# Reordering the start of a fused FFT filter and feed-forward kernel: first-FFT copies, load order, and the half-swaps of batch 1

## The chip, the cores and the metric

The kernel runs on one core of one Trainium2 chip. The metric is the device time of one execution in microseconds (us); lower is better. The engines are TensorE (PE, its weight loads apart as PEld), VectorE (DVE), ScalarE (ACT), GpSimd (POOL) and SyncE (SP, which here only issues transfers).

## The reference

An input x of shape (8, 3008, 256) is filtered along its second axis in the frequency domain, and every one of the 24064 resulting rows goes through a feed-forward block with a squared ReLU.

```python
X = np.fft.rfft(x, axis=1)                      # x: (8, 3008, 256)
Y = X * (filt_r + 1j * filt_i)[None, :, :]      # filter: (1505, 256)
y = np.fft.irfft(Y, n=3008, axis=1).reshape(24064, 256)
h = np.maximum(y @ w_in, 0.0)                   # w_in: (256, 2048)
out = h * h @ w_out                             # w_out: (2048, 256)
```

## The kernel before

**The transform.** The length 3008 is split as 64 x 47. One batch passes through stage A (a 47-point transform as matrix products with the constant in `sC0`), stage B (a 64-point transform with `sSB`, whose PSUM result is multiplied by the filter `sF` into `prod`), stage P (the inverse 64-point transform with `sSP`, copied to `ze` and written to the DRAM array `dZ`), and stage Y (the inverse 47-point transform of `zt`, which is read back from `dZ`, copied out as `yt`). Batches 1 to 7 also pass through a DRAM array `dU` between stages A and B, to bring another index onto the partitions. From batch 1 on, `unit_b` swaps the two halves of 64 partitions of `prod` by two copies into `yf`, and `unit_s` adds the other half of `prod` to it. For batch 1 these two copies run on POOL (lines 445 and 446), for batches 2 to 7 on DVE.

**The feed-forward block.** It works on 47 groups of 512 rows with 8 slots each. In a slot, `ffn_g1` multiplies `yt` by `sWin` into `psH` (line 542) and ACT applies the ReLU (line 546); DVE squares it (`ffn_sq`, line 550); `ffn_g2` multiplies an older group's `h` by `sWout` into `psO` (line 557). The FFT of batch 1 and later is spread over these slots by `fft_plan`, which gives each step a slot number `r` and a place in it. Batch 1 has `unit_b` in slots 14 to 33, `unit_p` two slots later, and also the rest of stage Y of batch 0. The last loop of the function writes the order out; every engine carries out its own instructions in this order, and each waits on semaphores for its operands and buffers.

**The prologue.** Before the first slot, batch 0 is transformed on its own. x of batch 0 is loaded in three parts (`load_wide`), cast to half precision (`cast_wide`), taken through stage A in turned form (`chunk_a0`, lines 395 to 405: eight steps, each with two PSUM banks `dt` 0 and 1), turned by products with an identity (`turn_u`, line 413, six steps), and the filter is brought into place by products with a selection matrix (`place_f`, lines 285 to 299, twelve steps, half of them after `turn_u` and mixed with stages B and P). A loop over `r` then does stages B and P of batch 0. `chunk_a` does three quarters of stage A of batch 1, and `unit_y(0, 0..3)` the first quarter of stage Y of batch 0, with which the first slots can start. `keep_warm` gives PE products of zeros while the first x loads.

**The queues.** Almost all transfers are issued by SP in program order; one that waits holds up all behind it. Each transfer also waits for the one eight places earlier, with which it shares a semaphore. The three `ze` buffers of a batch are reused: the fourth `ze` of batch 0 waits for the first write to `dZ`. The `prod` pool has three buffers, and the selection matrix `sPF` holds one of them until the filter is placed. PSUM tiles `psH`, `psF` and `psO` have two buffers each; a `psH` tile has two banks and counts as one tile for waits.

Of the kernel before, what the change touches and what calls it, by code (L numbers as in the profile page):

```python
# [111 lines left out]
def kernel(  # L112
# [9 lines left out]
    nc = tc.nc  # L122
# [10 lines left out]
    dPF = nc.inline_tensor(PF_np, name="cPF")  # L133
# [28 lines left out]
    def psO(name):  # L162
        return pps.tile([128, 2, 256], F32, tag="psO", name=name, bufs=2)

    def psH(name):
        return pps.tile([128, 2, 512], F32, tag="psH", name=name, bufs=2)
# [34 lines left out]


    sC0 = const.tile([128, 1472], F16, name="sC0")
    nc.scalar.dma_start(out=sC0, in_=dC0.ap())
    s0 = sC0[:, 0:576].rearrange("p (w q) -> p w q", q=96)
    s1 = sC0[:, 896:1472].rearrange("p (w q) -> p w q", q=96)
    sSA = sC0[0:94, 576:672]
    sSY = sC0[0:112, 672:766]
    ident = sC0[:, 768:896]
    sPF = p_prod.tile([128, 6, 128], F16, tag="prod", name="sPF")  # L210
    nc.scalar.dma_start(out=sPF, in_=dPF.ap().rearrange("p (w q) -> p w q", q=128))

    xw32, xw16 = {}, {}

# [6 lines left out]
        nc.sync.dma_start(out=t, in_=(v0[:, 0:8, :], v1, v0[:, 8:16, :])[k])  # L221
        xw32[(b, k)] = t

    def cast_wide(b, k, eng):
        t = p_x16.tile([128, 8, D], F16, tag="x16", name=f"xw16_{b}_{k}")
        for i in range(2):
            m = slice(4 * i, 4 * i + 4)
            eng.tensor_copy(out=t[:, m, :], in_=xw32[(b, k)][:, m, :])
        xw16[(b, k)] = t

    for k in range(3):
# [5 lines left out]
    def load_f(im):  # L237
        filt = filt_i if im else filt_r
        t = p_y.tile([128, QF], F32, tag="yt", name=f"f32_{im}")
        nc.sync.dma_start(out=t, in_=filt[0:1504, :].rearrange("a d -> (a d)")  # L240
                          .rearrange("(p e) -> p e", e=QF))
        f32s.append(t)

    load_f(0)
    load_f(1)
    nyq = p_out.tile([128, 2, D], F32, tag="ost", name="nyq")
    nc.gpsimd.memset(nyq, 0.0)
# [9 lines left out]
    zero = const.tile([128, 128], F16, name="zero")  # L257
    nc.vector.memset(zero, 0.0)

    def keep_warm(n):  # L260
        ps = psO("warm").rearrange("p a d -> p (a d)")
        for _ in range(n):
            nc.tensor.matmul(ps[:, 0:128], zero, zero, start=True, stop=True)

    nc.scalar.copy(out=zero[0:1, 0:1], in_=zero[0:1, 1:2])
    keep_warm(125)


    sF = const.tile([128, 2, NC, D], F16, name="sF")

    f16s = []

# [45 lines left out]
        nc.sync.dma_start(out=w32s[2][:, c, :],  # L318
                          in_=moe_w_out.rearrange("(jt r) c -> r jt c", r=128)[:, c, :])

    def cast_wout(k):
        c = slice(4 * k, 4 * k + 4)
        nc.gpsimd.tensor_copy(out=sWout[:, c, :], in_=w32s[2][:, c, :])


    x16s, us, uts, prods, zes, zts, yts = {}, {}, {}, {}, {}, {}, {}
# [57 lines left out]
    def chunk_a0(c):  # L384

        for k in range(2):
            for dt in range(2):
                if dt == 0:
                    banks, _ = bank_pair(f"psA_0_{c}_{k}")
                ps = banks[dt]  # L390
                for i in range(4):
                    m = 4 * k + i
                    o = ps[:, 96 * i:96 * i + 96]
                    d = slice(128 * dt, 128 * dt + 128)
                    nc.tensor.matmul(o, xw16[(0, 2 * (c % 2))][:, m, d], s0[:, c // 2, :],
                                     start=True, stop=False)
                    nc.tensor.matmul(o, xw16[(0, 1)][0:120, m, d], s0[0:120, 2 + c, :],
                                     start=False, stop=True)
                m = 32 * c + 16 * k
                o = uT[:, dt, :, m:m + 16].rearrange("p c (m q) -> p m c q", q=4)  # L400
                pv = ps[:, 0:384].rearrange("p (m c q) -> p m c q", m=4, q=4)
                if dt == 0:
                    nc.scalar.copy(out=o, in_=pv)
                else:
                    nc.vector.tensor_copy(out=o, in_=pv)
# [25 lines left out]
    def unit_b(b, p):  # L431
        ps = psF(f"psB_{b}_{p}")
        for i in range(2):
            nc.tensor.matmul(ps[:, i * D:(i + 1) * D], sSB[:, 2 * p + i, :],  # L434
                             uts[b][:, 2 * p + i, :], start=True, stop=True)
        prod = p_prod.tile([128, 2, 2, D], F16, tag="prod", name=f"prod_{b}_{p}")
        nc.vector.tensor_mul(  # L437
            out=prod,
            in0=ps.rearrange("p (a d) -> p a d", d=D).unsqueeze(1).to_broadcast([128, 2, 2, D]),
            in1=sF[:, :, 2 * p:2 * p + 2, :])  # L440
        prods[(b, p)] = prod
        if b > 0:
            yf = p_yf.tile([128, 2, D], F16, tag="yf", name=f"yf_{b}_{p}")
            swap = nc.gpsimd if b == 1 else nc.vector
            swap.tensor_copy(out=yf[0:64], in_=prod[64:128, 1])  # L445
            swap.tensor_copy(out=yf[64:128], in_=prod[0:64, 1])  # L446
            prods[(b, p)] = prod, yf

    def unit_s(b, p):
# [39 lines left out]
                              in_=v[48 * k:48 * k + 48, 8 * c:8 * c + 8, :])  # L489
        zts[(b, c)] = zt  # L490

    yps = {}

    def unit_y(b, n):

        g, dt = divmod(n, 2)
        if n == 0:
            yts[b] = p_y.tile([128, 2, S], F16, tag="yt", name=f"yt_{b}")
        zt = zts[(b, g // 2)]
        if not prologue[0]:  # L500
            ps = psF(f"psY_{b}_{n}")
        elif g % 2 == 0:
            ps = psF(f"psY_{b}_{n}") if dt == 0 else psO(f"psY_{b}_{n}").rearrange("p a d -> p (a d)")
        else:
            if dt == 0:
                yps[0] = psH(f"psY_{b}_{n}")
            ps = yps[0][:, dt, :]
        if prologue[0]:
            for k in range(2):
                nc.tensor.matmul(ps[:, 128 * k:128 * k + 128], zero, zero, start=True, stop=True)  # L510
        for jj in range(4):
            nc.tensor.matmul(ps[:, 94 * jj:94 * jj + 94],  # L512
                             zt[:, 4 * (g % 2) + jj, dt * 128:(dt + 1) * 128],
                             sSY, start=True, stop=True)
        r, t = g // 2 * 2, g % 2 * 4
        o = yts[b].rearrange("p d (r a t) -> p d r a t", r=8, t=8)[:, dt, r:r + 2, :, t:t + 4]
        pv = ps[:, 0:376].rearrange("p (j a i) -> p i a j", j=4, i=2)
        if dt == 0:
            nc.scalar.copy(out=o, in_=pv)  # L519
        else:  # L520
            nc.vector.tensor_copy(out=o, in_=pv)  # L521
# [62 lines left out]
    def fft_plan(b):  # L584

        plan = {}

        def put(r, place, f, *a):
            plan.setdefault((r, place), []).append((f, a))

        if b == 1:
            for n in range(4, 16):
                put(n - 1 if n < 8 else 10 + n // 2 if n < 12 else 4 * n - 31, n % 2,
                    unit_y, 0, n)
        t0 = 2 if b == 1 else 6
        for a in range(12 if b == 1 else 0, 16):
            put(t0 + a // 2, a % 2, unit_a, b, a)
        put(10 if b == 1 else 14, 1, read_u, b)
        t0 = 14 if b == 1 else 18
        for p in range(12):  # L600
            r = t0 + 19 * p // 11
            put(r, 0, unit_b, b, p)
            put(r, 0, unit_s, b, p)
            put(r + 2, 1, unit_p, b, p)
        t0 = 36 if b == 1 else 40
        for c in range(4):
            put(t0, 1, read_z, b, c)
        if b + 1 < B:
            for c in range(2):
                put(t0 - 13, 1, load_x, b + 1, c)  # L610
            for c in range(4):
                r = t0 - 8 + 3 * c
                put(r, 1, cast_x, b + 1, c)
                if c < 2:
                    put(r, 1, load_x, b + 1, c + 2)
        for n in range(16):
            if b == 1:
                put(38 + n // 2 if n > 3 else 39, n % 2, unit_y, b, n)
            else:
                put(44 + n // 2, n % 2, unit_y, b, n)  # L620
        return plan
# [4 lines left out]


    uT = p_h2.tile([128, 2, NC, 128], F16, tag="h2", name="uT")
    for k, eng in enumerate((nc.vector, nc.vector, nc.gpsimd)):
        cast_wide(0, k, eng)  # L630

    def load_const(t, d, k):
        c = slice(12 * k, 12 * k + 12)
# [19 lines left out]
    uts[0] = p_ut.tile([128, NC, D], F16, tag="ut", name="ut_0")  # L653
    for k in range(6):
        turn_u(k)
    for k in range(3):
        if k == 2:
            load_wout(0)
        load_wide(1, k)
        cast_wide(1, k, nc.gpsimd)  # L660
    load_wout(1)
    for k in range(4):
        cast_wout(k)
    for k, eng in enumerate((nc.vector, nc.scalar, nc.vector)):
        place_f(0, k, eng)
    place_f(1, 0, nc.scalar)
    for r in range(14):
        if r < 12:
            unit_b(0, r)
        if r < 10 and r % 2 == 0:  # L670
            place_f(1, r // 2 + 1, nc.scalar)
        if r < 6 and r % 2 == 1:
            place_f(0, r // 2 + 3, nc.scalar)
        if r >= 2:
            unit_p(0, r - 2)
        if r == 10:
            read_z(0, 0, (0,))
    read_z(0, 1, (0,))
    for c in (0, 2, 1):
        chunk_a(1, c)  # L680
    for c in range(2):
        read_z(0, c, (1,))
    for c in (0, 2, 1):
        write_u(1, c)
    for n in range(4):
# [53 lines left out]
```

## Time and profile before

| quantity | value |
|---|---|
| median of 5 runs | 821.2 us (817.61 to 822.67) |
| profiled execution, its own time | 819.99 us |
| its span in the profile | 818.2 us |
| PE busy | 787.7 us (96%) |
| DVE busy | 543.4 us (66%) |
| ACT busy | 554.2 us (68%) |
| POOL busy | 39.0 us (5%) |
| first ReLU of the feed-forward block (ACT, line 546) | 61.51 us from the span's start |
| the chain that ended last, by engine | PE 82%, DMA 10%, DVE 4%, POOL 2%, ACT 1% |

The profile is one execution, 1.8 us of whose time lies outside the span. "Busy" is the time in which an engine has an instruction under way. Where a row of a view ends in brackets, it gives the idle time of the engine before the instruction and what ended that idle time. A "window" is a stretch of the span in us from its start; the granted clock (PEclk) is the share of the full clock that TensorE had in it.

### The profile page before, as it was taken

To read this page: it belongs to the slowest core of one execution; us is meant where nothing else is said; L and a number is where in the kernel's file an instruction comes from. 1 tells how busy PE (TensorE), PEld (TensorE's weight loads), DVE (VectorE), ACT (ScalarE), POOL (GpSimd) and SP (SyncE) were. 2 spreads that over 40 slices of the span, in tenths; PEclk is the share of its full clock that TensorE was granted. 3 is DMA by queue.
4 is the path that set the end of the run, shared out by engine and by line. 5 is a ranking of instruction groups with operands and counts; after the bars stand their busy time and mean duration, and the time that the engine had idled before them with its cause. 6 is when DMAs were issued, how large, how long until landed. Compare 5 with 4: busy or idle time off the path is not lost.

```text
span 818.2 us, 14996 instructions
## 1 busy us (share of the span) xinstructions
PE 787.7 (96%) x6201; PEld 559.4 (68%) x6201; DVE 543.4 (66%) x868; ACT 554.2 (68%) x709; POOL 39.0 (5%) x53
## 2 busy tenths in 40 slices
PE   7879898999999999999999999999999999999998
PEld 7745565666677676776768667676767667676666
DVE  5755567558965699557985599656995579653442
ACT  2747565677777677676777767776776767766664
POOL 3520221000000000000000000000000000000000
PEclk9999999999999999999999999999999999999999
DMA  9893255534672554424572455715555242411111
GB/s 364 344 270 96 76 150 134 112 105 152 164 174 58 163 155 129 130 76 144 155 196 64 107 162 151 174 59 161 150 135 127 79 140 78 126 56 39 39 40 52
DMA packets 87948, 108.11 MB, mean 132 GB/s; under 512 B 6224, under 2 KB 78544, under 8 KB 83408
## 3 DMA queue, kind: packets, MB, share of 16 engines
q1 hardware_dynamic: 87528, 106.59, 45.3%
q8 instruction: 48, 0.79, 0.4%
q10 hardware_dynamic: 288, 0.57, 0.3%
q14 instruction: 20, 0.16, 0.1%
q0 software_dynamic: 64, 0.00, 0.0%
HBM read 58.90 MB, written 48.23 MB: 131 GB/s over the span
## 4 chain that ended last, share of the span: by engine, by line
PE 82%; DMA 10%; DVE 4%; POOL 2%; ACT 1%; issue 0%; ACTq 0%; POOLq 0%; DVEq 0%; SPq 0%
PE psO L557 36%; PE psH L542 35%; DMA ut<-dU 3%; DMA dZ<-ze 3%; PE psA L351 3%; PE psY L512 3%; PE psB L434 2%; PE psP L470 2%; DMA sSB<-cSB 2%; DMA zt<-dZ 2%; DVE prod L437 2%; DVE h L550 1%; DMA sPF<-cPF 1%; POOL yf L446 1%; POOL yf L445 1%; ACT h L546 1%
## 5 line engine op out<-in xcount | busy, mean ns | idle before, releaser
L546 ACT ACTIVATE h<-psH 128x1024 f16<-128x1024 f32 x376 | 385.1, 1025 | 196.1 <-PE psH L542 196.1
L542 PE MATMUL psH<-yt,sWin 128*128 128x512 f16 (+7 forms) x1728 | 388.6, 352 | 3.9 <-DVE yt L521 3.4
L557 PE MATMUL psO<-sWout,h 128*128 128x256 f16 x3008 | 389.6, 273 | 0.3 <-DVE h L550 0.3
L557 PEld LDWEIGHTS <-h 128*128 128x128 f16 x3008 | 290.9, 98 | 79.0 <-DVE h L550 0.6
L550 DVE TENSOR_TENSOR h<-h 128x1024 f16<-128x1024 f16 x376 | 254.0, 685 | 104.8 <-ACT h L546 103.2
L542 PEld LDWEIGHTS <-sWin 128*128 128x128 f16 x1728 | 159.8, 98 | 104.6 <-issue 6.4
L437 DVE TENSOR_TENSOR prod<-psB,sF 128x1024 f16<-128x1024 f32 x96 | 116.7, 1220 | 12.1 <-PE psB L434 8.9
L472 ACT CAST ze<-psP 128x512 f16<-128x512 f32 x96 | 55.9, 586 | 29.8 <-PE psP L470 22.9
L521 DVE CAST yt<-psY 128x376 f16<-128x376 f32 x64 | 35.0, 549 | 57.0 <-PE psY L512 56.7
L357 DVE CAST u<-psA 96x512 f16<-96x512 f32 x50 | 34.3, 687 | 47.6 <-PE psA L351 45.1
L564 ACT COPY ost<-psO 128x512 f32<-128x512 f32 x94 | 55.4, 589 | 9.1 <-PE psO L557 7.7
L452 DVE TENSOR_TENSOR yf<-prod,yf 128x512 f16<-128x512 f16 x84 | 35.7, 425 | 19.4 <-POOL yf L446 17.0
L512 PEld LDWEIGHTS <-zt 112*128 112x128 f16 x512 | 34.7, 97 | 15.3 <-issue 5.0
L512 PE MATMUL psY<-sC,zt 112*128 112x94 f16 x512 | 42.2, 205 | 2.9 <-DMA zt<-dZ 1.9
L434 PE MATMUL psB<-ut,sSB 128*128 128x256 f16 x192 | 36.8, 273 | 3.2 <-DVE prod L437 1.2
L351 PE MATMUL psA<-x,sC 94*96 94x512 f16 x96 | 36.6, 382 | 0.0
L470 PE MATMUL psP<-yf,sSP 128*128 128x256 f16 x168 | 32.6, 276 | 4.2 <-DVE prod L437 3.6
L434 PEld LDWEIGHTS <-sSB 128*128 128x128 f16 x192 | 18.7, 98 | 24.3 <-issue 5.7
L519 ACT CAST yt<-psY 128x376 f16<-128x376 f32 x64 | 29.8, 467 | 1.5 <-issue 1.0
L330 DVE CAST x<-x 94x2048 f16<-94x2048 f32 x24 | 29.2, 1217 | 0.0
L355 ACT CAST u<-psA 96x512 f16<-96x512 f32 x50 | 28.6, 572 | 0.0
L445 DVE COPY yf<-prod 64x512 f16<-64x512 f16 x72 | 20.8, 289 | 2.5
(59 smaller groups left out, 248.2 us busy)
## 6 DMA issues: line engine op xcount, KB each, us to landing
x<-in_x_dram SPq DMA_DIRECT2D x20, 768.0 KB
dZ<-ze SPq DMA_DIRECT2D x32, 384.0 KB
zt<-dZ SPq DMA_DIRECT2D x64, 192.0 KB
dU<-u SPq DMA_DIRECT2D x28, 384.0 KB
out_dram<-ost SPq DMA_DIRECT2D x32, 256.0 KB
out_dram<-ost SPq DMA_DIRECT2D x64, 128.0 KB
ut<-dU SPq DMA_DIRECT2D x7, 1024.0 KB
xw<-in_x_dram SPq DMA_DIRECT2D x6, 1024.0 KB
```

The costliest lines, as they stand in the source:

```text
L351: nc.tensor.matmul(ps[0:96, :], sSA, x16s[(b, c)][:, m, :], start=True, stop=True)
L434: nc.tensor.matmul(ps[:, i * D:(i + 1) * D], sSB[:, 2 * p + i, :], uts[b][:, 2 * p + i, :], start=True, stop=True)
L437: nc.vector.tensor_mul(out=prod, in0=ps.rearrange("p (a d) -> p a d", d=D).unsqueeze(1).to_broadcast([128, 2, 2, D]), in1=sF[:, :, 2 * p:2 ...
L452: nc.vector.tensor_add(out=yf, in0=prod[:, 0], in1=yf)
L470: nc.tensor.matmul(ps[:, i * D:(i + 1) * D], sSP[:, c2, :], prod[:, i, :], start=True, stop=True)
L472: nc.scalar.copy(out=zes[(b, c)][:, 2 * i6:2 * i6 + 2, :], in_=ps.rearrange("p (a d) -> p a d", d=D))
L512: nc.tensor.matmul(ps[:, 94 * jj:94 * jj + 94], zt[:, 4 * (g % 2) + jj, dt * 128:(dt + 1) * 128], sSY, start=True, stop=True)
L542: nc.tensor.matmul(ps[:, i, o:o + n], sWin[:, dt, jt * 128:(jt + 1) * 128], yts[b][:, dt, r:r + n], start=(dt == 0), stop=(dt == 1))
L546: nc.scalar.activation(out=h2[:, 2 * s:2 * s + 2, :], in_=ps, func=AF.Relu)
L550: nc.vector.tensor_mul(out=v, in0=v, in1=v)
L557: nc.tensor.matmul(pso[g][:, t % 2, :], h2s[g][:, jt, t * 128:(t + 1) * 128], sWout[:, jt, :], start=(jt == 0), stop=(jt == NJT - 1))
L564: nc.scalar.copy(out=ost, in_=pso[g])
```

## The change

The change has these parts:

- **Loads at the start.** The first transfer on ACT's queue carries only the 576 columns of `sC0` that `chunk_a0` reads. `sPF` and the other columns of `sC0` (identity and the constants of later stages) go to SP's queue, between the two halves of the filter.
- **Warm-up.** 26 products with 512 columns take the place of 125 with 128; DVE clears the operand first.
- **`cast_wide(0, 2)`.** DVE casts the first half and POOL the second; before, POOL cast both.
- **`chunk_a0`.** Where both banks are in one `psH` tile, both are copied out by the same engine (ACT and DVE in turn); before, ACT copied bank 0 and DVE bank 1 of every tile.
- **`turn_u` and `place_f`.** The first three steps of `place_f` come after steps 3, 4 and 5 of `turn_u`, on DVE, ACT and DVE; before, they came after the whole of `turn_u`.
- **Loads of x of batch 1 and of W_out.** These were issued before the writes of `dZ`; now they are issued in the loop over `r`, at r = 4, 7 and 10, and the second half of W_out after the reads of `zt` 0 and 1.
- **`cast_wout`.** The second half of W_out is cast by DVE in slots 4 and 5; before, POOL cast all of it.
- **`unit_y` in the prologue.** All four products use `psF` and `psO` tiles; before, two of them shared one `psH` tile.
- **Half-swaps.** The two copies into `yf` run on DVE for batch 1 too.

```diff
-    nc.scalar.dma_start(out=sC0, in_=dC0.ap())
+    nc.scalar.dma_start(out=sC0[:, 0:576], in_=dC0.ap()[:, 0:576])
...
-    nc.scalar.dma_start(out=sPF, in_=dPF.ap().rearrange("p (w q) -> p w q", q=128))
...
-    def cast_wide(b, k, eng):
+    def cast_wide(b, k, *engs):
...
-            eng.tensor_copy(out=t[:, m, :], in_=xw32[(b, k)][:, m, :])
+            engs[i].tensor_copy(out=t[:, m, :], in_=xw32[(b, k)][:, m, :])
...
     load_f(0)
+    nc.sync.dma_start(out=sPF, in_=dPF.ap().rearrange("p (w q) -> p w q", q=128))
+    nc.sync.dma_start(out=sC0[:, 576:1472], in_=dC0.ap()[:, 576:1472])
     load_f(1)
...
-    keep_warm(125)
...
+    nc.vector.memset(sF[:, 0, 0:2, :], 0.0)
+    ps = psO("warm").rearrange("p a d -> p (a d)")
+    for _ in range(26):
+        nc.tensor.matmul(ps, zero, sF[:, 0, 0:2, :], start=True, stop=True)
...
-    def cast_wout(k):
+    def cast_wout(k, eng):
...
         for k in range(2):
+            banks, groups = bank_pair(f"psA_0_{c}_{k}")
             for dt in range(2):
-                if dt == 0:
-                    banks, _ = bank_pair(f"psA_0_{c}_{k}")
...
-                if dt == 0:
+                if (pair_engine() is nc.scalar) if len(groups) == 1 else (dt == 0):
                     nc.scalar.copy(out=o, in_=pv)
...
-            swap = nc.gpsimd if b == 1 else nc.vector
-            swap.tensor_copy(out=yf[0:64], in_=prod[64:128, 1])
-            swap.tensor_copy(out=yf[64:128], in_=prod[0:64, 1])
+            nc.vector.tensor_copy(out=yf[0:64], in_=prod[64:128, 1])
+            nc.vector.tensor_copy(out=yf[64:128], in_=prod[0:64, 1])
...
-        elif g % 2 == 0:
+        else:
             ps = psF(f"psY_{b}_{n}") if dt == 0 else psO(f"psY_{b}_{n}").rearrange("p a d -> p (a d)")
-        else:
-            if dt == 0:
-                yps[0] = psH(f"psY_{b}_{n}")
-            ps = yps[0][:, dt, :]
...
+            for k in range(2, 4):
+                put(2 + k, 1, cast_wout, k, nc.vector)
...
-    for k, eng in enumerate((nc.vector, nc.vector, nc.gpsimd)):
-        cast_wide(0, k, eng)
+    for k in range(3):
+        cast_wide(0, k, nc.vector, nc.gpsimd if k == 2 else nc.vector)
...
         turn_u(k)
-    for k in range(3):
-        if k == 2:
-            load_wout(0)
-        load_wide(1, k)
-        cast_wide(1, k, nc.gpsimd)
-    load_wout(1)
-    for k in range(4):
-        cast_wout(k)
-    for k, eng in enumerate((nc.vector, nc.scalar, nc.vector)):
-        place_f(0, k, eng)
+        if k > 2:
+            place_f(0, k - 3, nc.vector if k % 2 else nc.scalar)
     place_f(1, 0, nc.scalar)
...
             unit_p(0, r - 2)
+        for k in {4: (0, 1), 7: (2,)}.get(r, ()):
+            load_wide(1, k)
+            cast_wide(1, k, nc.gpsimd, nc.gpsimd)
         if r == 10:
             read_z(0, 0, (0,))
-    read_z(0, 1, (0,))
+            load_wout(0)
+            for k in range(2):
+                cast_wout(k, nc.gpsimd)
+    read_z(0, 0, (1,))
+    read_z(0, 1)
     for c in (0, 2, 1):
         chunk_a(1, c)
-    for c in range(2):
-        read_z(0, c, (1,))
+    load_wout(1)
     for c in (0, 2, 1):
         write_u(1, c)
```

## The prediction

> **What bounds the kernel now.** I read the page first (PE 96% busy, and DVE, POOL and DMA all in the chain that ended last), then the windows, and cut the span where stages begin. Columns: window, length, then busy time and count of PE, PEld, DVE, ACT, POOL, then granted clock, DMA share, GB/s.
>
> ```profile
> 82.80:136.15 53.35, 44.34 (x309) 29.45 (x308) 33.05 (x48) 29.95 (x39) 13.46 (x22) 0.94 0.37 103
> 187.80:226.85 39.05, 39.05 (x283) 27.51 (x282) 37.62 (x66) 28.68 (x36) 0.00 (x0) 1.00 0.50 142
> ```
>
> Each is the stretch from the first to the last `prod` of one batch, 19 slots: batch 1, then batch 2. Batch 2 keeps PE busy throughout; batch 1 needs 14.3 us more and leaves PE idle for 9. DVE's timeline shows why (start, duration, then the idle time before in brackets):
>
> ```profile
> 82.80 1.23 DVE L437 TENSOR_TENSOR prod<-psB,sF 128x1024 f16<-128x1024 f32 x1 [0.38 <-PE psB L434]
> 85.46 0.43 DVE L452 TENSOR_TENSOR yf<-prod,yf 128x512 f16<-128x512 f16 x1 [1.44 <-POOL yf L446]
> 85.81 0.54 DVE L521 CAST yt<-psY 128x376 f16<-128x376 f32 x1
> ...
> 187.81 1.23 DVE L437 TENSOR_TENSOR prod<-psB,sF 128x1024 f16<-128x1024 f32 x1 [0.42 <-PE psB L434]
> 189.06 0.29 DVE L445 COPY yf<-prod 64x512 f16<-64x512 f16 x1
> 189.37 0.29 DVE L446 COPY yf<-prod 64x512 f16<-64x512 f16 x1
> 189.69 0.42 DVE L452 TENSOR_TENSOR yf<-prod,yf 128x512 f16<-128x512 f16 x1
> 190.03 0.68 DVE L550 TENSOR_TENSOR h<-h 128x1024 f16<-128x1024 f16 x1
> ```
>
> In batch 1 DVE stands still while POOL swaps: 3.01 us from `prod` to the next instruction, against 2.22 us with the swaps on DVE. DVE's lateness holds PSUM buffers, and so PE. The clock follows (length, PE busy and count, granted clock, DMA share, GB/s):
>
> ```profile
> 46.30:50.10 3.80, 0.00 (x0) 1.00 1.08 327
> 50.10:54.00 3.90, 3.90 (x13) 0.56 0.62 173
> 88.10:90.40 2.30, 0.02 (x1) 1.00 0.37 114
> 91.20:95.00 3.80, 3.80 (x20) 0.55 0.02 4
> 145.90:147.20 1.30, 0.19 (x2) 1.00 1.02 195
> 147.20:151.00 3.80, 3.28 (x42) 1.00 1.06 192
> ```
>
> After idle times of 3.8 and 2.3 us PE gets about half its clock for nearly 4 us; after 1.1 us it keeps it.
>
> In the prologue the end is set by transfers. SP's timeline, then the chain:
>
> ```profile
> 31.23 2.80 SPq L221 DMA_DIRECT2D xw<-in_x_dram  x2
> 39.19 7.84 SPq L475 DMA_DIRECT2D dZ<-ze  x3
> ```
> ```profile
> 39.19 10.17 DMA dZ<-ze
> ...
> 51.35 3.31 DMA dZ<-ze
> 54.68 3.27 DMA zt<-dZ
> ```
>
> The first `dZ` write lands at 49.36 behind 4 MB of loads; the fourth `ze` waits for it, its write lands at 54.68, `zt` is there at 57.95, and the first ReLU starts at 61.51.
>
> **Prologue: up to the first `dZ` write.** ACT's queue loses 0.43 MB that shared the engines with x. At the 0.42 MB/us of this stretch the second x part lands 1.0 us earlier; its cast ended at 11.23, so about 10.2. The new warm-up ends at about the same time: 12 products of 128 columns per us up to 6.2 us and 22 per us after make 16000 columns in 8.4 us, so 13312 need about 7.2 from 3.2, about 10.4. `chunk_a0` starts near 10.45 instead of 11.53. Its copies gain nothing: by the built program's waits, bank 1's product still waits for bank 0's copy (four stalls of 0.57 us now), and DVE copies in 0.56 us where ACT needs 0.48, so two tiles lose 0.08 each. The last `uT` copy ends at about 20.1 instead of 21.0. The casts of x part 2 end about 2 us earlier and hide.
>
> Mixing `turn_u` with `place_f` makes chains through the two `psH` buffers: a copy (ACT 1.0, DVE 1.23) must end before each product group (0.43 or 0.87). Walked with these rows and 0.25 from product to copy, the first stage P product comes 12.0 us after the last `uT` copy; now it is 11.5 (21.06 to 32.53). So -0.95 + 0.5 = -0.45 there (bounds -1.2 and +0.3). The loop over r is then PE's 1.53 us per step in both. The third `ze` copy, now ending at 37.39, ends at about 37.0.
>
> **Prologue: the queue.** SP now stands at the first `dZ` write from about 21 to 37.0, and the x loads, issued from 31.23 before, stand behind it: the queue that now runs dry only from 29.8 to 32.9 does so until about 38.5. In front of the fourth `dZ` write then go 3 x 0.39 MB of `dZ`, 3 x 1.05 of x, 0.2 of `zt` and 1.05 of W_out, 5.57 MB, and itself 0.39: 16.3 us at the 0.366 MB/us of 33 to 50, with a gap of 0.3, because the third x load waits for POOL's cast of the first (land 43.0, cast 2.03, issue 45.1). The write lands at about 55.8 instead of 54.68: +1.1 (bounds -0.5 and +2.5). The stall of the fourth `ze` (4.7 us on ACT) goes, but buys nothing, as the transfers in front of its write are late next. `chunk_a(1, 1)` needs the third x part (landed 49.5, cast by 51.6) and is done by 53.5, so PE idles for about 5 us before `unit_y`, where 0.28 idled before. By the rows above it gets half clock: four `unit_y` and the first `psH` group take 2.6 us longer, less 0.56 for the wait between the third and fourth `unit_y` that the new tiles remove and what the copies hide: the first ReLUs come 0.75 later against `zt` (bounds 0 and 1.7).
>
> **W_out on DVE.** Its two casts (0.65 each, from the 0.69 row of L228) stand in DVE's queue before the copy of `psY` 7, for which slot 8's product waits. That copy ended at 69.02, 0.4 before it was needed; with 1.3 more, less the time that DVE waited for ACT, slot 8 is 0.55 later (bounds 0 and 1.3). The transfer itself lands at about 62.5, before DVE reaches it. On POOL, its other half hides.
>
> **Batch 1.** I walked slots 14 to 35 with PE's 0.87 per product group of the feed-forward block, 0.22 per stage B or P, 0.17 per `unit_y`, and DVE's 2.22 per unit, 0.60 per square, 0.46 per `yt` copy, 1.13 per x cast. DVE needs 12 x 0.79 = 9.5 us less; about 1.4 of it becomes idle time in slots 16 to 20, where PE is late next, and the late parts at slots 16 and 29 shrink: the product of slot 16 waits for `yt` until 88.8 instead of 90.4, and PE idles 1.6 instead of 2.3; at slot 29 it idles 1.7 instead of 3.6. With the clock kept in both, the last stage P product of batch 1 ends at 131.4 instead of 139.8: -8.4. One bound is batch 2's own length plus `unit_y` (39.05 + 8 x 0.17 + 4 x 0.46 = 42.3): -11. The other, DVE's shorter units with the clock lost twice as now: a loss is 3.8 x 0.45 = 1.7, so -5.
>
> [...]
>
> **Sum.** +1.1 + 0.75 + 0.55 - 8.4 = -6.0. The -0.45 is inside the +1.1. Slots after batch 1 are unchanged and PE-bound, so it reaches the end. Against the profiled execution's 819.99 that is 814.0; the median of the runs is 1.2 above it. I forecast 814.5.
>
> **The rivals.**
> - *Batch 1 like batch 2, and the queue no later than now:* -11 + 0.55, about 810. For it: the 39.05 us window. Against it: batch 1 carries stage Y of batch 0 as well, whose copies hold `psF`.
> - *The clock is lost in both shortened gaps, and the queue reaches its worse bound:* -5 + 2.5 + 0.75 + 0.55 = -1.2, about 819, within 0.3%. For it: 1.6 us lies between the kept 1.1 and the lost 2.3.
> - *Slower: the second half of W_out is late.* It is issued only after the `zt` reads, and DVE stands at its cast in slot 4 with the squares and the copy of `psY` 7 behind it, for which slot 8 waits. Landing after about 69 us each us costs one; from 75 on the gain of 6 is gone; at 80 the time is about 825. Against it: its place in the queue at 57 and 5 us to land, as x took from 31.23 to 36.2.
> - *Stage A's copies are not freed.* This the waits show, and it is in the sum.
>
> **How the numbers follow.** Forecast 0.62, first rival 0.2, second 0.1, slower 0.08. A measurement of this kernel tells some 0.3% (2.5 us) from no change: faster means under 818.7. The forecast's tail and part of the second rival fall inside 0.3%: faster 0.83, same 0.1, slower 0.07. The range reaches from 808.5 (below the first rival) to 819.5 (the second rival with the bound of one more cost).
>
> **What would show it.** Right: no POOL row after about 57 us; `prod` to next instruction 2.22 us in batch 1, whose window is about 45 us; the first ReLU at about 63.5; first `dZ` write issued near 37; clock near 0.55 after the first `unit_y`, and 1.00 through slots 16 to 32. Wrong: a batch 1 window above 48 us, a wait of DVE for W_out in slots 4 and 5, or a first ReLU before 61 or after 66.

## The result and the profile after

The changed kernel takes 816.97 us (median of 49 runs, 815.18 to 819.91) against 820.0 us of the kernel before (median of 91 runs on the same chips): a ratio of 0.9967, 95% interval [0.9959, 0.9975]. That is about 3 us less, where the forecast stood 6.7 us below the median of the runs shown before: the direction and the range hold, the gain is less than half of the forecast. The profiled execution took 817.3 us, its span 815.5 (818.2 before). All ratios here and below are over fast runs: one run of `swaps_only` (832.65 us) and the profiled run of `x_early` (4549 us) were slow and are left out, which is why `x_early` was run once more for a profile.

Where the 2.7 us of the spans come from is read from the start of the ReLU of each slot in the two traces (after minus before):

| at the ReLU of slot | 0 | 8 | 9 | 15 | 17 | 29 | 34 | 374 |
|---|---|---|---|---|---|---|---|---|
| us | +5.51 | +5.48 | +5.79 | +5.79 | +2.98 | +1.45 | -2.55 | -2.71 |

So the prologue loses 5.5 us, W_out on VectorE 0.3, batch 1 wins 8.3, and the slots behind it win another 0.2 in sum. Batch 1 went as forecast and the prologue did not.

**Batch 1.** The windows of the changed kernel (columns as in the prediction's first fence), first to last `prod` of batch 1, and VectorE's timeline at its first unit:

```profile
88.68:133.34 44.66, 40.38 (x306) 28.26 (x305) 39.93 (x69) 29.60 (x39) 0.00 (x0) 1.00 0.44 123
```
```profile
88.68 1.22 DVE L434 TENSOR_TENSOR prod<-psB,sF 128x1024 f16<-128x1024 f32 x1 [0.47 <-PE psB L431]
89.94 0.29 DVE L441 COPY yf<-prod 64x512 f16<-64x512 f16 x1
90.24 0.29 DVE L442 COPY yf<-prod 64x512 f16<-64x512 f16 x1
90.56 0.43 DVE L448 TENSOR_TENSOR yf<-prod,yf 128x512 f16<-128x512 f16 x1
90.90 0.54 DVE L511 CAST yt<-psY 128x376 f16<-128x376 f32 x1
```

The window is 44.66 us where it was 53.35, POOL has nothing in it, the clock is 1.00 throughout, and from `prod` to the next instruction VectorE needs 2.22 us.

**Prologue.** SP's timeline (start, duration of the issue, line, transfer) and, after it, the chain of waits of the changed kernel (start, duration, what; followed back from the last instruction to what released it):

```profile
37.61 0.38 SPq L471 DMA_DIRECT2D dZ<-ze  x1
38.09 1.26 SPq L220 DMA_DIRECT2D xw<-in_x_dram  x2
41.16 0.38 SPq L471 DMA_DIRECT2D dZ<-ze  x1
45.68 0.33 SPq L220 DMA_DIRECT2D xw<-in_x_dram  x1
46.10 0.39 SPq L471 DMA_DIRECT2D dZ<-ze  x1
49.09 0.34 SPq L484 DMA_DIRECT2D zt<-dZ  x1
49.52 0.39 SPq L316 DMA_DIRECT2D wout<-in_moe_w_out_dram  x1
49.96 3.58 SPq L471 DMA_DIRECT2D dZ<-ze  x1
```
```profile
49.96 9.87 DMA dZ<-ze
...
59.85 3.18 DMA zt<-dZ
...
67.02 1.03 ACT h L536
```

The fourth `dZ` write, for which the last ACT copy was ready at 48.08, is issued behind the first half of W_out and takes 9.87 us to land, at 59.83. Before, it was issued later (51.35), took 3.31 and was there at 54.66. Everything in front of the first slot now hangs on this write. The windows show what the transfers did meanwhile (the last two numbers are DMA share and GB/s), first the kernel before in the stretch from which the prediction took its rate, then the changed kernel:

```profile
33.00:50.00 17.00, 11.59 (x106) 9.51 (x104) 11.87 (x10) 11.06 (x17) 9.29 (x10) 1.00 1.03 364
```
```profile
33.00:37.60 4.60, 4.60 (x48) 4.16 (x47) 3.57 (x3) 4.56 (x7) 0.63 (x1) 1.00 0.00 0
40.00:57.00 17.00, 12.25 (x66) 7.24 (x65) 9.11 (x9) 8.63 (x15) 6.08 (x6) 0.90 1.00 322
57.00:59.90 2.90, 0.59 (x5) 0.20 (x3) 1.28 (x2) 0.16 (x1) 1.01 (x2) 0.96 0.15 45
57.70:63.00 5.30, 0.00 (x0) 0.00 (x0) 0.66 (x2) 0.00 (x0) 2.03 (x2) 0.69 0.46 105
63.00:66.50 3.50, 3.37 (x25) 2.30 (x26) 1.10 (x2) 0.94 (x2) 0.00 (x0) 0.50 1.02 250
```

For 4.6 us before the first write nothing moves at all, then come 17 us of queue at 322 GB/s instead of 364, and at the end 2.9 us in which the transfer engines are busy for 15% of the time. The sizes of the packets tell the transfers apart (512 bytes for `dZ`, 1 KB for W_out): these 2.9 us move the last of the fourth write and, up to 58.24, of W_out. TensorE does nothing in the 5.3 us of the next window and the first `unit_y` at half clock (0.50).

### The profile page after: what moved, and what is told of

It is laid out like the page before. It is cut to its first block, busy times and chain, and to the rows that moved or that the text cites. A ratio compares the mean times of both kernels' runs of the same rounds, so it can differ in the third digit from the quotient of the medians.

```text
span 815.5 us, 14776 instructions
## 1 busy us (share of the span) xinstructions
PE 786.0 (96%) x6102; PEld 554.2 (68%) x6102; DVE 552.7 (68%) x896; ACT 554.3 (68%) x709; POOL 22.0 (3%) x26
## 4 chain that ended last, share of the span: by engine, by line
PE 87%; DMA 7%; DVE 3%; ACT 2%; issue 0%; POOL 0%; SPq 0%; ACTq 0%; POOLq 0%
PE psO L547 37%; PE psH L532 36%; PE psA L349 3%; PE psY L502 3%; PE psB L431 2%; DMA dZ<-ze 2%; PE psP L466 2%; DMA zt<-dZ 2%; DMA ut<-dU 1%; DMA xw<-in_x_dram 1%; PE warm L267 1%; DVE prod L434 1%; DVE h L540 1%; ACT h L536 0%; PE psf L283 0%; PE psf L286 0%
## 5 line engine op out<-in xcount | busy, mean ns | idle before, releaser
L431 PEld LDWEIGHTS <-sSB 128*128 128x128 f16 x192 | 18.6, 98 | 23.7 <-issue 5.1
L441 DVE COPY yf<-prod 64x512 f16<-64x512 f16 x84 | 24.3, 290 | 2.9
```

## The experiments

The theory after this reading: the half-swaps give 8.3 us on their own; the prologue loses 5.5 because the loads that were moved behind the first `dZ` write stand in front of the fourth one, W_out above all. Rivals: the swaps' gain needs the late prologue; or the write is late by its own straggling end, and W_out fills time that is lost anyway. Ratios are to the kernel before, on the same chip. Inside the prologue single profiles are compared, and there from the issue of the first `dZ` write on, because its start differs by a us or so from one execution to the next ("The start", further down).

### One part alone: `swaps_only`

```diff
 (kernel before)
-            swap = nc.gpsimd if b == 1 else nc.vector
+            swap = nc.vector
```

> The kernel before, with the half-swaps of batch 1 on VectorE and nothing else. Theory: from slot 14 to slot 36 the ReLUs of the changed kernel won 8.3 us on those of the kernel before, and this edit alone makes all of it: prologue and first ReLU as before (61.5 us), batch 1 window 45 us instead of 53.35, time 8.3 us shorter, ratio 0.990. Rival: part of the 8.3 us is slack that the late prologue left (the reads of dU and zt come earlier against the slots), and without that the edit wins 5 to 6 us, ratio 0.993 to 0.994.

Measured: ratio 0.990 [0.9882, 0.9918], 8 us less. In the trace the first ReLU is at 62.00 (+0.49) and the ReLU of slot 34 at -7.93, so that 8.4 us come between them. The window of batch 1, from the first `prod` to the end of the last, is 45.90 us (45.88 in the changed kernel, 54.57 before). The swaps' gain needs nothing else of the change, and they alone do more than the whole change.

### That part undone: `swaps_back`

```diff
 (changed kernel)
-            nc.vector.tensor_copy(out=yf[0:64], in_=prod[64:128, 1])
-            nc.vector.tensor_copy(out=yf[64:128], in_=prod[0:64, 1])
+            swap = nc.gpsimd if b == 1 else nc.vector
+            swap.tensor_copy(out=yf[0:64], in_=prod[64:128, 1])
+            swap.tensor_copy(out=yf[64:128], in_=prod[0:64, 1])
```

> The changed kernel with the half-swaps of batch 1 back on GpSimd. Theory: first ReLU stays at 67.0 us, the late first slots (5.5 us) and the W_out casts on VectorE (0.3 us) are all that is left, time 5.5 us longer than before, ratio 1.0067. Rival: the slots of batch 1 have slack to take some of the delay in (its own stalls come from transfers and not from VectorE), and the time is within 2 us of before, ratio 1.000 to 1.0025.

Measured: ratio 1.0054 [1.0033, 1.0075], 4.4 us more. The rest of the change is a loss, and batch 1 does not take it in: +4.35 at slot 0, +5.55 at slot 34. The first ReLU is at 65.86 here and not at 67.02: the first `dZ` write was issued 1.1 us earlier (36.55), which is the spread of the start that all profiles together show ("The start", below).

### W_out out of the way: `wout0_later` and `wout0_half`

```diff
 (changed kernel; wout0_half leaves half of this load in place and issues the other half after chunk_a)
         if r == 10:
             read_z(0, 0, (0,))
-            load_wout(0)
-            for k in range(2):
-                cast_wout(k, nc.gpsimd)
     read_z(0, 0, (1,))
     read_z(0, 1)
+    load_wout(0)
+    for k in range(2):
+        cast_wout(k, nc.gpsimd)
```

> The changed kernel with the first half of W_out loaded after the zt reads of chunks 0 and 1 instead of at r = 10, ahead of the fourth dZ write. Theory: the fourth write stands behind 1.05 MB less; at the 0.32 MB/us of 40 to 57 us it lands 3.3 us earlier, 56.6 instead of 59.85, first ReLU at 63.7 instead of 67.0, time 3.3 us shorter than the changed kernel, ratio to before 0.9925. Rival: the write waits for its own data and for engines that lag (from 57 to 59.85 us fewer than 4 of 16 moved anything), so W_out only fills time: it lands at most 1 us earlier, first ReLU at 66 or later, ratio 0.9955 or more.

> The changed kernel with only half of the first half of W_out (0.52 MB) ahead of the fourth dZ write, the other 0.52 MB after the zt reads. From the first dZ write's issue to the landing of the fourth it was 22.24 us in the changed kernel and 17.95 in wout0_later. Theory: bytes in front of the write set its landing, so half of them costs half: 19.8 to 20.4 us. Rival: it is the place in the queue and not the bytes (a transfer of any size ahead of the write makes lagging engines serve it late): over 21.5 us, or under 18.5 if a small one fits into gaps.

Measured: `wout0_later` has ratio 0.9922 [0.9900, 0.9945]. The chain of waits of `wout0_later`:

```profile
48.74 5.78 DMA dZ<-ze
...
54.59 3.04 DMA zt<-dZ
```

From the issue of the first `dZ` write to the landing of the fourth it takes 36.59 to 54.52, 17.9 us. With the whole 1.05 MB in front it was 22.2 us in the changed kernel's profile, 21.9 in that of `swaps_back` and 21.1 in that of `keep_clock`, which have the same queue. So the 1.05 MB cost 3.2 to 4.3 us, one profile of `wout0_later` against three; their bytes at the 322 GB/s of the window would be 3.3. The rival, that W_out only fills lost time, falls. With half of them in front (`wout0_half`: 36.55 to 57.12; 815.58 us in its one run) it is 20.6, which is 2.7 above 17.9, a little over the 19.8 to 20.4 expected: the cost grows with the bytes, but not quite in proportion, and how much of it is the straggling end is not separated.

The first ReLU is at 61.59, earlier than the 63.7 expected; 1.0 us of that is an earlier start of this execution (first `dZ` write at 36.59 instead of 37.61). At slots 8 and 9 `wout0_later` then loses 1.1 us against the kernel before, where the changed kernel lost 0.3. GpSimd's timeline in the changed kernel and in `wout0_later`, then VectorE's in the latter:

```profile
58.88 2.03 POOL L321 CAST sWout<-wout 128x1024 f16<-128x1024 f32 x2 [2.49 <-DMA wout<-in_moe_w_out_dram]
```
```profile
63.71 2.88 POOL L321 CAST sWout<-wout 128x1024 f16<-128x1024 f32 x2 [9.23 <-DMA wout<-in_moe_w_out_dram]
```
```profile
63.56 0.69 DVE L540 TENSOR_TENSOR h<-h 128x1024 f16<-128x1024 f16 x1 [0.22 <-ACT h L536]
64.78 2.35 DVE L540 TENSOR_TENSOR h<-h 128x1024 f16<-128x1024 f16 x2 [0.53 <-ACT h L536]
```

Beside each other GpSimd's two casts take 2.88 us instead of 2.03, and VectorE's two squares 2.35 instead of 1.38 (2 x 0.69).

### x of batch 1 back in front: `x_early`

```diff
 (wout0_later)
+    for k in range(2):
+        load_wide(1, k)
+        cast_wide(1, k, nc.gpsimd, nc.gpsimd)
     place_f(1, 0, nc.scalar)
     for r in range(14):
...
-        for k in {4: (0, 1), 7: (2,)}.get(r, ()):
-            load_wide(1, k)
-            cast_wide(1, k, nc.gpsimd, nc.gpsimd)
+        if r == 4:
+            load_wide(1, 2)
+            cast_wide(1, 2, nc.gpsimd, nc.gpsimd)
```

> As wout0_later, and the first two parts of x of batch 1 are issued before the loop over r (they wait for GpSimd's casts of W_in only, about 31 us, when the transfers are idle), the third after the first dZ write. Theory: what delays the start is the bytes in front of the fourth dZ write; with none there its write follows the fourth ze copy (48.1 us), takes 3.3 us as the lone write of the kernel before did, lands at 51.5, zt is there at 54.8, first ReLU at about 58.3 (8.7 us earlier than in the changed kernel), time about 8.5 us shorter than that, ratio to before 0.986. Rival: stage A of batch 1 on TensorE (chunk_a, done at 57.7 us in the changed kernel, 58.2 in the one before) is late next, it stands before unit_y in TensorE's order: first ReLU at 60 to 61, ratio about 0.989.

> x_early once more, for its profile. Theory: first ReLU at 58 to 59 us, 1 us given back at slots 8 and 9. Rival: first ReLU at 60 to 61, held by stage A of batch 1.

Measured: ratio 0.987 [0.9847, 0.9892]; the profiled run of the same kernel, `x_early_again`, took 808.47 us. The x loads are issued at 31.12 and 33.6, when nothing else moves. The fourth write is issued at 47.51 and has landed at 50.9, in 3.4 us; from the issue of the first write it is 14.1 us, another 3.8 less than in `wout0_later`, so the two x loads that were in front of it cost about as much as W_out (one profile of each). The first ReLU is at 57.94, 9.1 us earlier than in the changed kernel and 3.6 earlier than before. That is the theory's number, not the rival's: stage A of batch 1 ends at 52.0, before `zt`. Then W_out is late next. The chain of waits of `x_early_again`:

```profile
52.72 11.57 DMA wout<-in_moe_w_out_dram
...
64.31 0.69 DVE sWout L321
```

VectorE stands at its casts until the second half of W_out has landed, and slot 8 comes 1.4 us later. This is the slower rival of the prediction with its mechanism; in the changed kernel it did not happen, the casts ran at 72.2 without a wait.

### W_out elsewhere: `dz_first`, `split_wout`

Both are `x_early` with the two halves of W_out issued elsewhere:

- `dz_first`: the first half after the second `dZ` write, the second half after the third; all cast by GpSimd.
- `split_wout`: the first half after the second `dZ` write, cast by GpSimd; the second half after the reads of `zt` 0 and 1, cast by VectorE.

> As x_early, and the two halves of W_out go into the stretches in which the transfers would be idle: the first behind the second dZ write, the second behind the third; GpSimd casts both before the first slot, nothing of W_out is on VectorE. Theory: x and the first half of W_out land before the fourth ze copy (about 47.5 us), the fourth dZ write then stands behind 1.4 MB at most and lands at 51 to 53 us, first ReLU at 58 to 59, and the 0.8 to 1.2 us that wout0_later lost at slots 8 and 9 (GpSimd's casts beside VectorE's squares, 1.44 us instead of 1.04 and 0.69) are not there: time 2 us shorter than x_early, ratio to before 0.984. Rival: the second half of W_out costs the fourth write as much as the first did in the changed kernel (3 to 4 us): ratio 0.988 or more.

> As x_early, with the first half of W_out behind the second dZ write (as in dz_first, cast by GpSimd) and the second half after the zt reads of chunks 0 and 1 (as in the changed kernel, cast by VectorE in slots 4 and 5). Theory: 1.05 MB less stands in the queue after the zt reads, so the second half lands at about 58 us instead of 64.3 and VectorE need not wait for it: first ReLU at 58, and the 1.4 us that x_early_again lost at slot 8 fall to the 0.3 us of the casts themselves; time about 807 us, 1 us shorter than x_early, ratio to before 0.985. Rival: the first half of W_out delays the third or fourth dZ write as the second one did in dz_first: first ReLU at 60 or later.

Measured: `dz_first` 0.9916 [0.9899, 0.9933], the rival: with both halves of W_out in front, the second by 0.5 us, the fourth write lands 8.0 us after its issue, 4.6 later than in `x_early_again`. The chain of waits of `dz_first`:

```profile
47.83 8.02 DMA dZ<-ze
```

`split_wout` 0.9894 [0.9876, 0.9912]: no better than `x_early`, against the expectation. In its profile the fourth write takes 5.73 us, and with the same queue in the next kernel 3.97, against 3.4 in `x_early_again`. Though the first half of W_out is issued 3.4 us ahead of the third write, its last packets move at 50.97 and 48.42, after the issue of the fourth (48.36 and 47.59). It is thus in the way of that write; but in the first of the two profiles the write needs 3.1 us more when W_out is through, so how much of the 0.6 to 2.3 us is W_out's and how much the write's own slow end is not separated. In the three orders that were tried, one half of W_out lands too late (`x_early`) or stands in front of a `dZ` write.

### The clock: `keep_clock`, `split_wout_clock`

```diff
 (changed kernel: 20 products; split_wout: 8 products)
+    ps = psO("warm2").rearrange("p a d -> p (a d)")
+    for _ in range(20):
+        nc.tensor.matmul(ps, zero, sF[:, 0, 0:2, :], start=True, stop=True)
     for n in range(4):
         unit_y(0, n)
```

> The changed kernel with 20 products of zeros (512 columns each) between stage A of batch 1 and the first unit_y, where TensorE idled for about 5 us and then ran at half clock. From the landing of the fourth dZ write to the first ReLU it was 7.17 us (6.83 before). Theory: with the clock at 1.00 there it is 6.2 us, about 1 us shorter. Rival: the chain there is transfer and copies, and the clock costs nothing: 6.8 us or more.

> split_wout with 8 products of zeros (1.8 us) in TensorE's gap before the first unit_y (52.0 to 54.1 us in x_early_again, after which the clock was 0.5 for 3.4 us). Theory: the clock is kept and the first ReLU comes 1 us earlier, at 57; time 1 us shorter than split_wout, ratio 0.984. Rival: the gap is filled but the products end after zt is there, or the slots behind lose it again: no gain.

The chain of waits of `keep_clock` (813.98 us in its one run):

```profile
57.79 3.33 DMA zt<-dZ
61.17 0.34 PE psY L502 x4
...
63.89 1.03 ACT h L536
```

From the landing of the write (57.77) to the first ReLU it is 6.1 us, against 7.2 in the changed kernel (59.83 to 67.02): half clock there costs 1.1 us, one profile against one. In `split_wout_clock` the clock is 1.00 from 7.4 us to the end and the first ReLU is at 57.34, but the ratio is 0.9896 [0.988, 0.9913], no other than without the products. The profiled run (807.84 us) was the quickest of its four, the others took 810.62 to 811.48; what they lost where is open.

### The mixed order: `split_wout_clock_unmixed`

```diff
 (split_wout_clock)
         turn_u(k)
-        if k > 2:
-            place_f(0, k - 3, nc.vector if k % 2 else nc.scalar)
+    for k, eng in enumerate((nc.vector, nc.scalar, nc.vector)):
+        place_f(0, k, eng)
```

> split_wout_clock with the first three steps of place_f after the whole of turn_u, as in the kernel before (VectorE, ScalarE, VectorE). Theory: from the end of the last uT copy to the first stage P product it is 11.5 us as before and not 12.0 as in every run of the mixed order, so the mixing itself costs 0.5 us. Rival: the 0.5 us come from another part (copies of stage A, place of sPF), and it stays at 12.0.

Measured: from the last `uT` copy to the first stage P product 11.52 us, as in the kernel before (11.53); with the mixed order it is 12.00 to 12.01 in nine profiles. The one run took 808.5 us.

## Why the prediction was off

Of the prediction's own signs, the window of batch 1, the 2.22 us and the clock there came as said, and one sign of being wrong came too: the first ReLU after 66 (67.02). That the time lies in the range is partly luck: its upper end was made of clocks lost in batch 1, which were kept, and of a queue term of +2.5, where it came to +5.2.

**Batch 1: right.** The forecast was -8.4 us, the slots show -8.34, and `swaps_only` 8.4. The two idle times of TensorE that the walk left, 1.6 and 1.7 us, are 1.64 and 1.56 in the trace, and the clock is kept in both. That it is kept was the author's estimate, which no row or run before the result shows: the prediction's rows had 1.1 us kept and 2.3 lost, and nothing between. The trace after has it at 1.00 through both gaps (the last section has what went with it). The window came out at 44.66 against "about 45".

**The queue: the step that failed.** What waits for what was right, the fourth `dZ` write behind the loads; the term's size was wrong. It was +1.1 us (bounds -0.5 and +2.5), and the fourth write landed 5.2 us later than before, at 59.83 instead of the forecast 55.8. The 4.0 us between are made of these:

- *The rate.* 5.96 MB were to move at 0.366 MB/us, the rate of another stretch with other transfers in it. They moved at 0.32: from 38.4 to 57.0 us, 18.6 us instead of 16.6, that is 2.0 more. Why this stretch was slower no run shows.
- *The end.* The rest of the 18.8 us from issue to landing was 2.2 us for start and end. It took 0.8 to start and 2.85 to end, 1.4 us more: a sum of bytes by rate leaves out how the last of them straggle, and the reader of `dZ` waits for the last one. In the trace the last packets of the write end at 59.43, it has landed at 59.83, and the `zt` read behind it is issued at 59.85; the transfer engines are busy for 15% of the 2.9 us before. Part of this is chance of the execution: 155 of the write's 768 packets move in its last 2.9 us here, but 540 and 693 in `swaps_back` and `keep_clock`, with the same queue, where the write landed 0.3 and 1.1 us sooner after the first one's issue.
- *The start.* The first write was issued at 37.61 instead of 37.0. The mix of `turn_u` and `place_f` cost the 0.5 us that the walk gave, but `chunk_a0` began at 11.14 instead of 10.45, only 0.45 earlier than before, because the clock rose at 8.47 us (6.22 in the profile before) and the warm-up of products ran at half clock for longer (from product to product 0.43 us before the rise, 0.22 after it). With this warm-up the clock rose between 5.3 and 8.6 us in ten profiles and `chunk_a0` began between 9.6 and 11.2: this piece of the difference is chance of the execution too. (The prediction's 12 and 22 warm-up products per us count products that reach over a window's edge: 125 of them took 8.4 us, as it says, but at these rates they would take 7.1. Its 10.4 follows from the 8.4. And of the loads ahead of the first `dZ` write some 2.7 MB were still to move at its issue, not 4; no term rests on that.)

More telling than the sizes: the first half of W_out was counted among the bytes (1.05 of 5.96 MB, 2.9 us at the prediction's rate), and its place ahead of the write was seen, but only the second half was made a rival. What the first half costs was never set against an alternative: 3.2 to 4.3 us. And the upper bound of +2.5 has no working in the prediction; rate, end and start all went the same way, to +5.2.

**The clock before the first `unit_y`: mechanism right.** TensorE idled 5.5 us and got half clock (0.50 from 59.67 to 66.50), as forecast. The stretch behind grew by 0.34 us (6.85 to 7.19) against the forecast 0.75. By `keep_clock` the clock costs 1.07, where the prediction had 2.6 less what hides. With full clock in both, the stretch goes from 6.85 to 6.12; that the new PSUM tiles give these 0.7 is argued from the wait of 0.56 that they remove, and no run changes them alone.

**W_out on VectorE: right in kind.** +0.3 us between slots 8 and 9, against 0.55 (bounds 0 and 1.3). The same 0.3 shows in `keep_clock` and `swaps_back`; in `dz_first`, where GpSimd casts all of W_out, it is 0.0.

**Stage A's copies:** not freed, as the waits said; the rows of 0.57 to 0.65 us in which TensorE waits for a copy of `uT` are still there.

Measured, the terms are +5.2, +0.3, +0.3 and -8.3, together -2.5 (the table has -2.55 at slot 34); the spans differ by 2.7.

## What to carry to other kernels

Before a load is moved behind a write, ask which later write it then stands in front of: a transfer that nobody waits for yet delays the one for which everybody waits, here by 3.2 to 4.3 us for 1.05 MB. Look for the stretch in which the queue is empty, here the 7 us from 31 to 38, and put the loads there: two x loads there and W_out behind the `zt` reads made the first ReLU 9.1 us earlier. When a sum takes bytes by a rate, take the rate of a stretch like the one to come, and add the end of the last transfer as a term of its own, with a bound for it.

## What the runs showed of the hardware beyond that

In these traces the length of the one gap does not tell whether TensorE's clock is kept after idle time. Gaps of 1.64 and 1.56 us in batch 1 kept it and a gap of 1.83 us in `wout0_later` (46.66) did too; gaps of 2.00 and 2.10 us before the first `unit_y` lost it in `wout0_later` and `x_early_again`, and in the changed kernel a gap of 1.43 us at 47.67, just after smaller ones, was followed by half clock from 49.4 to 52.9.

How busy TensorE was in the stretch before goes with it better. The traces list the clock piece by piece: in the changed kernel it was full for 40.960, half for 3.413, full for 6.827, half for 6.827 and full for 747.519 us from the first rise (at 8.47) to the last fall. These are 12, 1, 2, 2 and 219 times 3.4133 us (to 0.01 us), and in the other profiles, too, the pieces between these two points are whole multiples of it; half clock came in pieces of 3.4, 6.8 or 10.2 us. Cut into steps of that measured length from the first rise on, the twelve profiles that have a record of the clock (all but that of `x_early`) show no exception: after each of the 22 steps at full clock in which TensorE was busy, as the profile counts it, for 43% or less, the clock was halved; after each of the 2781 with 48% or more it was kept. It came back after the 14 steps with 87% or more, and not after the 8 with 79% or less. In the kernel before these are 3 steps with 34% or less and 230 with 53% or more, in the changed kernel 2 with 43% or less and 230 with 63% or more. This is a count over the profiles of this case; what in the chip makes it so no run shows. Four of these steps (columns as in the prediction's first fence): one in the changed kernel, two in `wout0_later` (after its gap of 1.83 began, and with its gap of 2.00), one in `swaps_back`:

```profile
46.02:49.43 3.41, 1.46 (x10) 0.80 (x9) 0.77 (x1) 1.22 (x3) 1.43 (x2) 1.00 1.03 316
```
```profile
47.38:50.80 3.42, 2.31 (x11) 1.24 (x11) 0.91 (x2) 1.07 (x2) 2.02 (x2) 1.00 0.96 314
54.21:57.62 3.41, 1.47 (x8) 0.68 (x6) 1.28 (x2) 1.03 (x2) 0.27 (x1) 1.00 0.64 139
```
```profile
91.66:95.07 3.41, 1.64 (x15) 1.24 (x15) 2.11 (x3) 0.77 (x2) 1.20 (x2) 1.00 0.07 17
```

The first and the third (1.46 and 1.47 of 3.41 us busy, 43%) lost the clock; the second (68%; the gap of 1.83 lies across two steps) and the fourth (48%) kept it. In the changed kernel the steps with the gaps of batch 1 have 66% or more.

GpSimd's casts of W_out and VectorE's squares took longer when they ran at the same time: by 42% and 70% in `wout0_later` (2.88 for 2.03, 2.35 for 1.38 us), and again in `x_early_again` (a cast of 1.49 us instead of 1.04 beside squares of 0.98 and 1.44 instead of 0.69). In the other profiles, where the casts end before the first square, no cast took over 1.04 us and no square over 0.76.
